# A transformer-block kernel: the identity made on GpSimd, query weights in finer slices, transposes moved by one matmul, and one queue's order fixed

## The chip, the cores and the metric

The kernel runs on one core of one Trainium2 chip. The metric is device time in microseconds (us) of one execution. Every run was in the fast state, with a mean granted TensorE clock of 0.999 to 1.000; only the start is at half of it. "Engine names" below are those of the profile: PE is TensorE's matmul, PEld its weight load, DVE is VectorE, ACT is ScalarE, POOL is GpSimd and SP is SyncE, whose queue issues most loads. Times inside an execution count from the start of the profiled span; one execution takes about 1.8 us longer than its span.

## The reference, cut to what matters

A block in bf16 over 2048 tokens of width 1024: a layer norm, attention over 8 keys at a stride of 2 with 32 heads, a residual, then a second layer norm and a gated MLP with a spatial mix.

```python
def _A_ref(x, wqkv, wo):                       # x (1, 2048, 1024), wqkv (1024, 3072)
    qkv = (x @ wqkv) ...                       # queries, keys, values; 32 heads of 32
    ...                                        # 8 keys at distances 0, 2, .., 14; softmax
    return o @ wo
def _B_ref(x, w_in, w_sp, b_sp, w_out): ...    # gelu, layer norm, spatial mix, product
x = A_x
h = x + _A_ref(_layernorm(x, axis=-1), A_wqkv, A_wo)
h2 = h + _B_ref(_layernorm(h, axis=-1), B_w_in, B_w_sp, B_b_sp, B_w_out)
return h2
```

Its first step: normalize x, multiply by the query part of `wqkv`, then by the key part, then by the value part.

## The kernel before

The tokens are cut into 16 tiles of 128 (`x tile 0` to `x tile 15`) and four chunks of four tiles. In the first chunk each tile is loaded, normalized on VectorE, transposed on TensorE (eight 128x128 transposes against an identity matrix), copied from PSUM to SBUF by ScalarE and then multiplied by wq in 16 matmuls of 512 columns. After the queries of the four tiles come the key matmuls and the value matmuls of the chunk. What the change touches:

```python
NWARM = 11
XAT = (12, 13, 10, 0)       # the next tile's transposes go in front of this matmul of tile 0, 1, 2
...
csb = cpool.tile([P, 416], BF16, name="csb")
dma_w(csb[:, 0:128], consts_d.ap()[:, 0:128])          # dma_w: a load issued by GpSimd
ident = csb[:, 0:128]
...
wps = ps_att.tile([P, CH], FP32, name="wps", tag="L")  # 11 matmuls on zeros, to get the clock up
for _ in range(NWARM):
    T.matmul(wps[:], warm[:, 0:P], warm[:], start=True, stop=True)
...
dma(xts[0][:, 0:CH], x2d[0:P, 0:CH])                   # dma: a load issued by SP
A.dma_start(xts[0][:, CH:D], x2d[0:P, CH:D])           # and by ScalarE
A.dma_start(xts[1], x2d[P:2 * P, :])
for k0 in range(0, KT, 2):                             # wq: four loads of two slices, 512 KB each
    dma(wsb[0][:, k0:k0 + 2, :], wq_view[:, k0:k0 + 2, 0:D])
load_x(2)
load_x(3)
dma(csb[:, 128:416], consts_d.ap()[:, 128:416])
dma(wsb[1][:], wq_view[:, :, D:2 * D])                 # wk
for i in range(TPC, 2 * TPC):
    load_x(i)
...
def xpose(i, xn, *parts):                              # cut: tile 0's first part shares ring "L" with wps
    ...
            T.transpose(tps[i][:, a, :], xn[:, a * P:(a + 1) * P], ident)
    for k0, k1 in parts:
        A.copy(xnT[0][:, k0:k1, i * P:(i + 1) * P], tps[i][:, k0:k1, :])
...
ln(0)                                                  # stats, sqrt, reciprocal, normalize of tile 0
for part in ((0, 2), (2, 5), (5, KT)):
    xpose(0, xns[0], part)
ln(1)
for i in range(TPC):
    acc = new_acc()
    for n, (nh, kt) in enumerate([(nh, kt) for kt in range(KT) for nh in range(2)]):
        if n == XAT[i] and i + 1 < TPC:
            xpose(i + 1, xns[i + 1], (0, 4), (4, KT))
        T.matmul(acc[:, nh, :], xnT[0][:, kt, i * P:(i + 1) * P], wsb[0][:, kt, nh * CH:(nh + 1) * CH],
                 start=(kt == 0), stop=(kt == KT - 1))
    if i + 2 < TPC:
        ln(i + 2)
    ...
    qt_ = nc.sync.dma_start_transpose(...)             # the query tile, transposed by a DMA on SP's queue
tc.add_manual_dep(dma(wsb[2][:], ...wv...).ins, qt_.ins.name, ...)   # wv behind the query transposes
```

TensorE, ScalarE and VectorE run this part in the order in which it is written. The order of SP's queue is chosen by the scheduler of the framework when the kernel is built.

## Time and profile before

| | value | read from |
|---|---|---|
| time | 723.02 us, median of 3 (722.82 to 723.10) | timed runs |
| span of the profiled run | 720.9 us | the page |
| PE busy | 716.6 us, 99% | the page, part 1 |
| first transpose of x tiles 0, 1, 2, 3 | 6.19, 9.62, 13.74, 17.19 us | timeline of PE |
| first query, key, value matmul | 7.02, 22.39, 36.20 us | timeline of PE |
| landing of the identity | 6.02 us | semaphore events of the DMA |
| landing of wq's four loads | 5.76, 7.31, 8.65, 10.01 us | the same |
| landing of x tile 2 | 10.69 us | the same |

First, busy times (share of the span, number of instructions) and the chain that ended last, from the page of the kernel before:

```profile
PE 716.6 (99%) x3449; PEld 364.2 (51%) x3449; DVE 412.1 (57%) x442; ACT 236.3 (33%) x301; POOL 64.1 (9%) x78
...
PE 99%; DVE 0%; DMA 0%; ACT 0%; issue 0%
```

TensorE is the limit, and it has almost no idle time after the start. Near 203.5 us TensorE waits for VectorE's `oT`, by 0.09 us in this profile.

The chain of waits of the kernel before (start us, duration us, what):

```profile
0.74 2.68 DMA xp<-in_A_x_dram
...
5.54 0.65 DVE xn L253 x2
6.18 0.00 issue
6.19 0.37 PE tp_152 L265 x2
6.56 0.55 PE tpa L265 x6
7.10 2.68 PE acc L303 x12
...
13.90 0.45 PE tpa L265 x8
14.35 0.66 PE acc L303 x3
15.01 0.02 issue
15.02 2.33 PE acc L303 x10
```

The chain passes x tile 0's load and its normalization and then stays on PE. The normalized part was there at 5.88, the last warm-up matmul had drained (ended) at 6.13, and the identity had landed at 6.02. The identity's own load is this line of GpSimd's timeline (start, duration, engine, line, operation, what it waited for):

```profile
1.22 0.70 POOL L168 DMA_DIRECT2D csb<-qt_consts  x1 [0.77 <-POOLq L938]
```

Issued at 1.22, landed at 6.02: 4.8 us on the way.

The only other loss is behind x tile 2's transposes. PE's weight loads there (start, busy us, operation; in brackets the idle time and what ended it):

```profile
13.52 0.65 PEld L265 LDWEIGHTS <-xn 128*128 128x128 bf16 x8
14.13 0.37 PEld L303 LDWEIGHTS <-xnT 128*128 128x128 bf16 x3
15.02 0.98 PEld L303 LDWEIGHTS <-xnT 128*128 128x128 bf16 x6 [0.52 <-ACT xnT L267]
```

Three matmuls of the tile in hand follow the eight transposes (L265); the next weight load belongs to tile 2 and waits for ScalarE's copy of those transposes. The matmul behind it starts 0.193 us later than its predecessor's columns need (512 columns take 0.216 us in these traces). I call it the copy stall.

And two lines of VectorE, the statistics and the normalization of x tile 2:

```profile
10.71 0.69 DVE L241 BATCH_NORM_STATS2 bnst<-xp 128x6 f32<-128x512 bf16 x1 [1.70 <-DMA xp<-in_A_x_dram]
...
12.87 0.55 DVE L253 TENSOR_SCALAR xn<-xp,mv_72,rstd_73 128x1024 bf16<-128x1024 bf16 x1
```

The normalized tile is ready at 13.41.

### The profile page before, as it was taken

How to read it: one execution, taken by the hardware profiler on the slowest of the kernel's cores; microseconds unless marked ns; L12 is line 12 of the kernel's file. 1: busy time of each engine (PE TensorE's matmuls, PEld its weight loads, DVE VectorE, ACT ScalarE, POOL GpSimd, SP SyncE). 2: the span in 40 equal slices, each digit the busy share in tenths (PEclk: the TensorE clock that was granted, in tenths of full speed). 3: DMA queues.
4: the chain of work that ended last, by engine and by line, in shares of the span. 5: the costliest groups of instructions: out<-in, count | busy, mean ns of one | idle time of the engine just before them, and what ended most of it. 6: DMA issues, size and time to landing. Idle time of an engine off the chain costs nothing.

```text
span 720.9 us, 8469 instructions
## 1 busy us (share of the span) xinstructions
PE 716.6 (99%) x3449; PEld 364.2 (51%) x3449; DVE 412.1 (57%) x442; ACT 236.3 (33%) x301; POOL 64.1 (9%) x78
## 2 busy tenths in 40 slices
PE   9999999999999999999999999999999999999998
PEld 4666665666544454445445444444444444444444
DVE  5898699979999999887961203222222222222222
ACT  4398452532447685766725520000000000000000
POOL 0010400012002302201114000000000000000000
PEclk9999999999999999999999999999999999999999
DMA  9986664567662842642337989363016301120002
GB/s 335 266 284 151 203 160 167 165 194 253 240 228 91 247 160 90 237 114 59 147 115 210 269 225 307 142 158 106 30 44 148 115 30 45 37 86 9 1 15 73
DMA packets 119990, 107.35 MB, mean 149 GB/s; under 512 B 72896, under 2 KB 98272, under 8 KB 119952
## 3 DMA queue, kind: packets, MB, share of 16 engines
q1 hardware_dynamic: 110624, 73.95, 34.8%
q0 software_dynamic: 7888, 31.43, 13.0%
q10 hardware_dynamic: 1440, 1.44, 0.8%
q8 instruction: 27, 0.44, 0.2%
q14 instruction: 11, 0.09, 0.0%
HBM read 55.09 MB, written 30.74 MB: 119 GB/s over the span
## 4 chain that ended last, share of the span: by engine, by line
PE 99%; DVE 0%; DMA 0%; ACT 0%; issue 0%
PE acc L901 27%; PE acc L393 21%; PE acc L741 13%; PE acc L791 13%; PE acc L923 13%; PE acc L669 8%; PE acc L303 2%; PE L L501 1%; DMA xp<-in_A_x_dram 0%; PE tpa L265 0%; DVE bnst L241 0%; DVE xn L253 0%; DVE bnst L242 0%; DVE ot L925 0%; PE tp_152 L265 0%; ACT sd_145 L247 0%
## 5 line engine op out<-in xcount | busy, mean ns | idle before, releaser
L741 PEld LDWEIGHTS <-hnT 128*128 128x128 bf16 x512 | 50.0, 98 | 47.3 <-issue 0.4
L923 PEld LDWEIGHTS <-zg 128*128 128x128 bf16 x462 | 45.2, 98 | 51.7
L449 DVE TENSOR_TENSOR prod<-qT,kT 128x4096 bf16<-128x4096 bf16 (+1 forms) x32 | 68.1, 2149 | 3.0 <-DMA kT<-qkv_d_58 1.5
L607 DVE TENSOR_TENSOR prod<-vT,AB 128x4096 bf16<-128x4096 bf16 (+1 forms) x32 | 64.3, 2022 | 0.8
L609 DVE TENSOR_TENSOR oT<-oT,prod 128x4096 bf16<-128x4096 bf16 (+1 forms) x32 | 64.5, 2017 | 0.1
L925 DVE TENSOR_TENSOR ot<-acc,hr 128x1024 bf16<-128x1024 f32 (+2 forms) x18 | 19.9, 1106 | 73.1 <-PE acc L923 73.1
L923 PE MATMUL acc<-wout_a,zg 128*128 128x512 bf16 (+1 forms) x264 | 58.2, 373 | 0.0
L741 PE MATMUL acc<-win_1453,hnT 128*128 128x512 bf16 x256 | 58.2, 379 | 0.0
L393 PE MATMUL acc<-xnT,wk 128*128 128x512 bf16 x256 | 56.3, 379 | 0.0
L791 PE MATMUL acc<-hnT,win_1657 128*128 128x512 bf16 x256 | 56.2, 379 | 0.0
L669 PE MATMUL acc<-wo_sb,oT 128*128 128x512 bf16 x256 | 56.1, 379 | 0.0
L393 PE MATMUL acc<-xnT,wv 128*128 128x512 bf16 x256 | 55.9, 379 | 0.0
L404 ACT CAST stg<-acc 128x1024 bf16<-128x1024 f32 x36 | 36.4, 1010 | 58.4 <-PE acc L393 54.6
L393 PEld LDWEIGHTS <-wk 128*128 128x128 bf16 x256 | 36.9, 145 | 18.6 <-issue 0.4
L393 PEld LDWEIGHTS <-wv 128*128 128x128 bf16 x256 | 37.0, 145 | 18.2
L923 PE MATMUL acc<-wout_b,zg 128*128 128x512 bf16 (+1 forms) x198 | 44.4, 373 | 0.0
L741 PE MATMUL acc<-win_1550,hnT 128*128 128x512 bf16 (+1 forms) x256 | 44.2, 326 | 0.0
L791 PE MATMUL acc<-hnT,win_1663 128*128 128x512 bf16 x192 | 42.4, 379 | 0.0
L393 PE MATMUL acc<-xnT,wq 128*128 128x512 bf16 x192 | 42.2, 379 | 0.0
L797 ACT ACTIVATE z1s<-acc 128x1024 bf16<-128x1024 f32 x28 | 28.5, 1019 | 37.2 <-PE acc L791 32.5
L669 PEld LDWEIGHTS <-oT 128*128 128x128 bf16 x256 | 25.0, 98 | 30.3 <-DVE oT L609 0.4
L791 PEld LDWEIGHTS <-win_1657 128*128 128x128 bf16 x256 | 24.9, 98 | 30.0 <-issue 0.4
(267 smaller groups left out, 969.0 us busy)
## 6 DMA issues: line engine op xcount, KB each, us to landing
z_d<-z1s SPq DMA_DIRECT2D x28, 256.0 KB, 2.6
z1c<-z_d SPq DMA_DIRECT2D x28, 256.0 KB, 2.7
z_d<-u SPq DMA_DIRECT2D x12, 448.0 KB, 2.5
xr<-in_A_x_dram SPq DMA_DIRECT2D x16, 256.0 KB, 2.6
h_d<-hb SPq DMA_DIRECT2D x16, 256.0 KB, 2.0
hr<-h_d SPq DMA_DIRECT2D x16, 256.0 KB, 2.8
out_dram<-ot SPq DMA_DIRECT2D x15, 256.0 KB, 2.0
kT<-qkv_d_58 POOLq DMA_DIRECT2D x3, 1056.0 KB, 8.7
```

The lines of the kernel that those rows point to most:

```text
L393: G["mmins", c, xi, dp] = T.matmul(G[key][:, j, :], wv[:, kt, dl, :], xnT[c][:, kt, :], start=(kt == 0), stop=(kt == KT - 1))
L404: A.copy(stg[:], G[key][:])
L449: V.tensor_tensor(qs[w]["prod"][:, d0:d1], qT[:, d0:d1], kT[:, d0:d1, o:o + CH], op=ALU.mult)
L607: V.tensor_tensor(dst[:, :, sq].rearrange("p d (q s) -> p d q s", q=nq), vv, abb, op=ALU.mult)
L609: V.tensor_tensor(oTs[c][:, :, sq], oTs[c][:, :, sq], pvs[w, q0][:, :, sq], op=ALU.add)
L669: T.matmul(st["acc", il][:, nh, :], oTs[c][:, dl, il * P:(il + 1) * P], wo_sb[:, dl, nh * CH:(nh + 1) * CH], start=(dl == 0), stop=(dl == ...
L741: T.matmul(accf[:, n0:n1], hnTs[c][:, il, kt, :], wins[hf][:, kt, n0:n1], start=(kt == 0), stop=(kt == KT - 1))
L791: T.matmul(G["accy", c, fp][:, j, :].rearrange("p (a b) -> p a b", a=TPC), wt[:, kt, f0 * P:(f0 + 1) * P], hnTs[c][:, :, kt, :], start=(kt ...
L797: A.activation(z1s[:], G["accy", c, fp][:], ACTF.Gelu_apprx_tanh)
L901: m_ = T.matmul(acc[:, j, :], z2sb[a][:, f * P:(f + 1) * P], wspT[:, a, :], start=(a == 0), stop=(a == NT - 1))
L923: T.matmul(acc[:, m0 - n0:m1 - n0], zg[:, f, il * P:(il + 1) * P], wt[:, f0, m0:m1], start=(f == 0), stop=(f == NF - 1))
L925: V.tensor_tensor(ot[:, n0:n1], acc[:, 0:n1 - n0], hr[:, n0:n1], op=ALU.add)
```

## The change

Its intent: make the identity on the chip, so that the first transposes need not wait for a load; have wq's later slices land one by one, so that an earlier start finds its weights; move tile 2's transposes one matmul forward, so that four matmuls cover the copy instead of three; and fix the order of SP's queue by explicit dependences.

```diff
-XAT = (12, 13, 10, 0)
+XAT = (12, 12, 10, 0)
...
-    dma_w(csb[:, 0:128], consts_d.ap()[:, 0:128])
     ident = csb[:, 0:128]
+    nc.gpsimd.memset(ident, 1.0)
+    nc.gpsimd.affine_select(ident, ident, [[-1, P]], ALU.is_equal, 0.0, base=0, channel_multiplier=1)
...
+    def turn(i_, j_):      # i_ comes behind j_ in its queue; no semaphore
+        tc.add_manual_dep(i_.ins, j_.ins.name, ...)
+        return i_
...
-    for k0 in range(0, KT, 2):
-        dma(wsb[0][:, k0:k0 + 2, :], wq_view[:, k0:k0 + 2, 0:D])
+    for k0, k1 in ((0, 2), (2, 4), (4, 5), (5, 6), (6, 7), (7, 8)):
+        dma(wsb[0][:, k0:k1, :], wq_view[:, k0:k1, 0:D])
...
+    wv_load = turn(dma(wsb[2][:], wq_view[:, :, 2 * D:3 * D]), qts[3])      # qts: the four query transposes
...
+                if c == 1:
+                    turn(G["xntr", c], wv_load)      # chunk 1's x transposes behind wv's load
...
+                if c == 0:
+                    turn(i_, G["kvhalo"])
...
-        for i in range(2 * TPC, NT - 2):
-            load_x(i)
-        x_slot(NT - 2)
-        x_slot(NT - 1)
-        dma(pairs[NT // 2 - 1][:], ...)              # only x tiles 14 and 15 in one load
+        for i in range(2 * TPC, 2 * TPC + 2):
+            turn(load_x(i), qts[2])                  # x tiles 8 and 9 behind the third query transpose
+        for i in range(2 * TPC + 2, NT, 2):          # x tiles 10 to 15: two to a load
+            ...
+            turn(dma(pairs[i // 2][:], ...), G["xntr", 1])
```

More of the change, by code (lines that the diff above doesn't have):

```diff
@@ L212, in load_x @@
         x_slot(i)
-        dma(xts[i], x2d[i * P:(i + 1) * P, :])
+        return dma(xts[i], x2d[i * P:(i + 1) * P, :])
+    def turn(i_, j_):
+        tc.add_manual_dep(i_.ins, j_.ins.name, mybir.DependencyInfo(mybir.DependencyClass.NoSync, mybir.DependencyReason.DATA),
+                          reason="order of one queue")
+        return i_
+    qts = []
     manual = {mybir.EngineType.PE, mybir.EngineType.Activation, mybir.EngineType.DVE}
@@ L309 @@
             A.copy(qs0[:, i], acc[:].rearrange("p a b -> p (a b)").rearrange("p (m dl) -> p dl m", dl=DLO))
-            qt_ = nc.sync.dma_start_transpose(att_in[0][0][:, :, i * P:(i + 1) * P], qs0[:, i])
-    tc.add_manual_dep(dma(wsb[2][:], wq_view[:, :, 2 * D:3 * D]).ins, qt_.ins.name,
-                      mybir.DependencyInfo(mybir.DependencyClass.NoSync, mybir.DependencyReason.DATA), reason="load wv behind the query transposes")
+            qts.append(nc.sync.dma_start_transpose(att_in[0][0][:, :, i * P:(i + 1) * P], qs0[:, i]))
+    wv_load = turn(dma(wsb[2][:], wq_view[:, :, 2 * D:3 * D]), qts[3])
     wo_sb = wtile([P, DLO, D], "wo_sb", "wB")
@@ L371, in tr @@
                     xnT[c] = xtp.tile([P, KT, CH], BF16, name="xnT", tag="xnT")
-                nc.sync.dma_start_transpose(xnT[c][:, :, il * P:(il + 1) * P], G["xn", c, il][:].rearrange("s (a p) -> s a p", p=P))
+                G["xntr", c] = nc.sync.dma_start_transpose(xnT[c][:, :, il * P:(il + 1) * P], G["xn", c, il][:].rearrange("s (a p) -> s a p", p=P))
+                if c == 1:
+                    turn(G["xntr", c], wv_load)
             trs.append(dma_op(4.0, tr, [n_] + ([G["qkvlast", c - 2]] if c >= 2 else []), free="xn"))
@@ L400, in ev @@
                         if dp == 3:
-                            dma(qkv_d[xi][:, :, CH - HALO:CH], att_in[0][xi][:, :, CH:CH + HALO])
+                            i_ = dma(qkv_d[xi][:, :, CH - HALO:CH], att_in[0][xi][:, :, CH:CH + HALO])
+                            G.setdefault("kvhalo", i_)
                     else:
@@ L652, in xr_load @@
                 st["xr", k] = bp.tile([P, D], BF16, name="xr", tag="xr", bufs=XRB)
-                dma(st["xr", k][:], x2d[(c * TPC + k) * P:(c * TPC + k + 1) * P, :])
+                i_ = dma(st["xr", k][:], x2d[(c * TPC + k) * P:(c * TPC + k + 1) * P, :])
+                if c == 0:
+                    turn(i_, G["kvhalo"])
         dma_op(0.0, xr_load, [G["avmid", c]])
@@ L822, in x_loads @@
     def x_loads():
-        for i in range(2 * TPC, NT - 2):
-            load_x(i)
-        x_slot(NT - 2)
-        x_slot(NT - 1)
-        dma(pairs[NT // 2 - 1][:], x2d[(NT - 2) * P:NT * P, :].rearrange("(a p) d -> p a d", p=P))
+        for i in range(2 * TPC, 2 * TPC + 2):
+            turn(load_x(i), qts[2])
+        for i in range(2 * TPC + 2, NT, 2):
+            x_slot(i)
+            x_slot(i + 1)
+            turn(dma(pairs[i // 2][:], x2d[i * P:(i + 2) * P, :].rearrange("(a p) d -> p a d", p=P)), G["xntr", 1])
     for c in range(1, NCH):
```

## The prediction

> **What bounds the kernel now.** TensorE alone. The page has PE busy 716.6 of 720.9 us at full clock; the chain of waits is 99% PE. In the trace, the only matmul after 6 us that starts over 0.1 us later than its columns need is one of 0.19 us (14.62 to 15.02, a weight load waiting for ScalarE's copy of x tile 2's transposes). From 22.4 us on TensorE hardly waits. So only the first 22 us can give anything; DVE, ACT and DMA later only have to keep pace.
>
> **What bounds the start (timeline and landings, 0 to 22 us).** Warm-up matmuls keep PE busy until about 5.93. The first normalized part of x tile 0 is ready at 5.88. But the identity, a GpSimd DMA issued at 1.22, lands 4.8 us later, at 6.02; PE's wait on it ends at 6.10, the first transpose starts at 6.19. So it is the last wait, by about 0.15 us. Behind it everything is tight: wq's four landings are 5.76, 7.31, 8.65 and 10.01; their first matmuls start at 7.02, 7.89, 8.76 and 10.07. The last two have 0.10 and 0.06 us of slack, so without the split an earlier start would be lost again.
>
> **What the change does.**
> - Identity by memset and select on GpSimd: takes 4.8 us off the path if done before about 5.9. GpSimd is free from about 0.7. A 128x4 power took it 1.04 us here; I estimate memset and 128x128 select at under 2 us, done by 3. Gain 0.15 us. It also takes 16 packets of 2 KB (84 ns each) out of a saturated DMA stream: later landings 0.08 us earlier.
> - wq's slices 4 to 7 one by one: 0.675 us of data each, landings near 7.9, 8.6, 9.25 and 9.9 for matmuls wanted near 8.6, 9.0, 9.9 and 10.3. No wait. Two more issues of 0.47 us on SP delay the issue of x tiles 2 and 3, but their data queue behind wq anyway (tile 2 landed 10.69, expected 10.6).
> - Tile 2's transposes one matmul (0.216 us) earlier: a fourth matmul then covers the ScalarE copy, and the 0.19 us stall goes. They want to start near 13.36; tile 2's normalized x is ready near 13.33, so they start near 13.45, against 13.74. First matmul of tile 2 near 14.77 instead of 15.02.
> - Order of the SP queue: the instruction lists show the same order; the only differences are paired loads of x tiles 10 to 13 and shifted semaphores. About 0.
>
> **Sum.** The first k matmul moves from 22.39 to about 22.14; the 0.25 us should survive, since VectorE's chain hangs on PE at 65.9 and 153.3 us (it waited 2.3 us for PE) and moves with it. PE waits for VectorE once, 0.08 us at 203.4: a late attention DMA could take some back. 723.02 - 0.25 = 722.77.
>
> **Would show it right:** first transpose near 6.0 with no wait for an identity; no excess between matmuls at 8.6 to 10.4; no stall after tile 2's transposes; last matmul 0.25 us earlier.
>
> **What would make it wrong.** The select follows a reconfiguration of GpSimd. The Trainium skill (GPSIMD Engine Reference, 2.1 Instruction dispatch) puts the first call of a freshly loaded kernel at about 6 us of invisible load; in this trace 21 us passed between reconfiguration and first call, so it shows neither yes nor no. If paid, the identity is ready near 7.5 and the kernel is 1 to 1.5 us slower (about 724.3); I give that 15%. Otherwise jitter of attention's DMAs, 0.2 us. Nothing reaches 2%.

## The result, and the profile after

The changed kernel took 722.64 us (median of 6 runs, 722.38 to 722.82), the kernel before 722.96 us in the same rounds (6 runs, 722.81 to 723.12). The ratio of the two is 0.9995 with a 95% interval of 0.9982 to 1.0008: "same" at the 2% level, as predicted. A ratio here is the mean time of one kernel's fast runs over the mean of the other's in the same rounds, so it is not quite the ratio of the medians that are quoted. The interval is wide beside what we look for; I use the means of several sets as well. In this set they differ by 0.34 us; in the repeat below, by 0.37 us. The two ranges of the first set do not overlap, so a gain of about a third of a microsecond looks real. 723 us hold 2000 times that, so this study is about where tenths of a microsecond go.

GpSimd's timeline of the changed kernel:

```profile
0.79 0.20 POOL L169 MEMSET csb<- 128x128 bf16 x1 [0.29 <-POOLq L951]
1.07 0.29 POOL L170 TENSOR_SCALAR_AFFINE_SELECT csb<-csb 128x128 bf16<-128x128 bf16 x1
```

The identity is finished at 1.36 instead of 6.02. The load of GpSimd's code that the prediction feared is not there: a reconfiguration instruction stands at 0.95, the select starts 0.12 us after it and takes 0.29 us. The Trainium skill (GPSIMD Engine Reference, 2.1 Instruction dispatch) says that the first call of a freshly loaded kernel pays about 6 us with no visible instruction; this trace shows no such time for this instruction. Why, no run here tells.

And yet the first transpose did not come sooner. The chain of the changed kernel:

```profile
5.62 0.65 DVE xn L261 x2
6.26 0.07 issue
6.33 0.39 PE tp_155 L273 x2
...
7.17 2.76 PE acc L311 x12
...
13.83 0.04 issue
13.86 0.62 PE tpa L273 x8
14.48 3.02 PE acc L311 x14
```

The first transpose is at 6.33, against 6.19. The trace names the reason: the first transposes share the PSUM buffer "L" with the warm-up matmuls, the warm-up drained at 6.18, and PE's wait on its own semaphore is recorded at 6.22 to 6.27. Tile 2's transposes start at 13.86, against 13.74 before. PE's weight loads and VectorE at the same place as shown of before:

```profile
13.86 0.45 PEld L273 LDWEIGHTS <-xn 128*128 128x128 bf16 x8 [0.53 <-DVE xn L261]
14.27 0.59 PEld L311 LDWEIGHTS <-xnT 128*128 128x128 bf16 x4
15.16 0.77 PEld L311 LDWEIGHTS <-xnT 128*128 128x128 bf16 x5 [0.30 <-ACT xnT L275]
```

```profile
11.10 0.69 DVE L249 BATCH_NORM_STATS2 bnst<-xp 128x6 f32<-128x512 bf16 x1 [2.01 <-DMA xp<-in_A_x_dram]
...
13.26 0.55 DVE L261 TENSOR_SCALAR xn<-xp,mv_73,rstd_74 128x1024 bf16<-128x1024 bf16 x1
```

The copy stall is gone: four weight loads follow the transposes, and the matmul at 15.16 starts when its predecessor allows (the 0.30 us of idle weight load are hidden behind a running matmul). But there is a new wait in front of the transposes: 0.53 us on the weight-load side, 0.198 us of it not hidden, for the normalized tile 2. That tile was loaded at 11.08. So the first profile says that the changed kernel is *later* at 22 us (first key matmul 22.54, before 22.39), while the times say that it is faster. The profiled executions themselves took 722.67 us (kernel before, under the lowest of its timed runs) and 722.79 us (changed kernel, above its median), so the two profiles show a quick execution of the one beside a slow one of the other. One profile of each kernel cannot settle tenths of a microsecond; repeats had to show what varies.

### The profile page after: what moved, and what is told of

It is laid out like the page before. It is cut to its first block, busy times and chain, and to the rows that moved or that the text cites. A ratio compares the mean times of both kernels' runs of the same rounds, so it can differ in the third digit from the quotient of the medians.

```text
span 721.1 us, 8406 instructions
## 1 busy us (share of the span) xinstructions
PE 713.3 (99%) x3388; PEld 364.0 (50%) x3449; DVE 412.1 (57%) x442; ACT 236.3 (33%) x301; POOL 62.3 (9%) x79
## 4 chain that ended last, share of the span: by engine, by line
PE 98%; issue 0%; DVE 0%; DMA 0%; ACT 0%
PE acc L914 27%; PE acc L402 21%; PE acc L803 13%; PE acc L753 13%; PE acc L936 13%; PE acc L681 8%; PE acc L311 2%; PE L L511 1%; DMA xp<-in_A_x_dram 0%; PE tpa L273 0%; DVE bnst L249 0%; DVE xn L261 0%; DVE bnst L250 0%; DVE ot L938 0%; PE tp_155 L273 0%
```

## The experiments

Eleven runs were made (nine variants, and both kernels again), in three sets on three chips, each in five rounds beside the kernel before. All were correct. Where I give a mean below, it is that of the five runs; their scatter is mostly about 0.2 us (standard deviation), so a mean is good to about 0.1 us, which is an estimate from that scatter. Apart from the first result, the changed kernel was in the first of the three sets alone, so most comparisons with it go across sets. Each variant has one profile, which is of one of its five runs, often the quickest or the slowest.

| kernel | median us | mean us | the kernel before, mean of the same set | ratio, 95% interval |
|---|---|---|---|---|
| before, repeated | 723.13 | 723.12 | 722.96 | 1.0002, 0.9990 to 1.0015 |
| changed, repeated | 722.55 | 722.59 | 722.96 | 0.9995, 0.9983 to 1.0008 |
| changed, identity loaded again | 722.69 | 722.82 | 722.96 | 0.9999, 0.9985 to 1.0012 |
| changed, without the fixed order | 723.96 | 724.12 | 722.96 | 1.0016, 1.0004 to 1.0029 |
| changed, tile 2's transposes at 13 again | 722.55 | 722.65 | 722.97 | 0.9997, 0.9984 to 1.0011 |
| changed, wq in four loads again | 722.88 | 722.86 | 722.97 | 0.9999, 0.9987 to 1.0012 |
| changed, warm-up in another buffer | 722.69 | 722.64 | 722.97 | 0.9996, 0.9984 to 1.0009 |
| changed, x tile 2 loaded in halves | 722.90 | 722.86 | 722.97 | 0.9999, 0.9987 to 1.0012 |
| changed, 13 warm-up matmuls | 722.57 | 722.58 | 723.05 | 0.9994, 0.9980 to 1.0008 |
| before, tile 2's transposes at 12 | 722.76 | 723.09 | 723.05 | 1.0001, 0.9988 to 1.0013 |
| changed, three steps more (below) | 722.22 | 722.24 | 723.05 | 0.9989, 0.9976 to 1.0001 |

### 1. Both kernels again

No edit. The labels are `before_again` and `after_again`.

> The kernel before, unchanged, as a control. Every theory: the same as the kernel before within 0.1 us. Its profile is a second sample of the start: how far the landings of x tile 0 (3.42 us in the first profile), the first two wq slices (5.76) and x tile 2 (10.69), and the start of the first k matmul (22.39), move from one execution to the next. If they move by 0.2 us or more, one profile can't settle differences of that size in the start.

> The changed kernel, unchanged. Its first profile showed the first transpose 0.15 us after the last warm-up matmul had drained (6.18 to 6.33), where the kernel before had 0.06 us (6.13 to 6.19), and x tile 2 landing at 11.08 instead of 10.69. Theory 1 (the prediction: the identity's landing was the last wait): the first transpose comes near 6.0 in this second profile. Theory 2 (rival: the last warm-up matmul is the last wait, because the transposes write the PSUM tile that the warm-up wrote): again about 0.15 us after the warm-up has drained, near 6.3. Time: 0.2 to 0.4 us below the kernel before.

Measured: 723.13 and 722.55 us (medians). The control missed its expectation of 0.1 us: its mean, 723.12, is 0.16 us above that of the same kernel in the same set (722.96), so a difference of that size between two means says little. The repeat of the kernel before found the identity landing at 6.64 instead of 6.02, the first transpose at 6.78 instead of 6.19 and the first key matmul at 22.94 instead of 22.39. So in this execution the identity really was the last wait, by half a microsecond (the warm-up had drained at 6.13); in the first profile the warm-up was at least as late. Landings of loads move by 0.6 us between executions of one kernel: wq's first load came at 5.76 in one and 6.42 in the other, x tile 2 at 10.69 and 11.26. The clock varies too: in the first profile of the kernel before the full clock is granted from 6.87 on, behind tile 0's transposes, which are slow there (0.83 us from the first of them to the first query matmul, 0.74 us in the repeat).

The repeat of the changed kernel had its warm-up done at 5.41, because the clock rose earlier, and its first transpose at 6.09, right behind the normalized part (6.04). But tile 2's transposes began at 13.96, and the chain of waits now names their cause itself:

```profile
4.42 6.75 DMA xp<-in_A_x_dram
11.18 0.02 issue
11.20 0.69 DVE bnst L249
...
13.36 0.56 DVE xn L261
13.92 0.05 issue
13.96 0.62 PE tpa L273 x8
```

This chain no longer passes PE's start at all. It comes from x tile 2's load (issued at 4.42, landed at 11.18) through the normalization to the transposes. That gave the theory that the next experiments test. I call it **the gate**: tile 2's transposes start at the later of two times.

- The gate: x tile 2's landing plus 2.79 us. The 2.79 us are the path on VectorE and ScalarE in the changed kernel: 13.86 minus 11.08.
- TensorE's own pace: the first query matmul plus 6.49 us of work (6.71 us where the transposes go in front of matmul 13, one matmul of 0.216 us more), plus TensorE's waits on the way.

The rival: the start passes to the end one to one, and the differences are what each part of the change saves on TensorE.

### 2. The identity loaded again

```diff
-    nc.gpsimd.memset(ident, 1.0)
-    nc.gpsimd.affine_select(ident, ident, [[-1, P]], ALU.is_equal, 0.0, base=0, channel_multiplier=1)
+    dma_w(csb[:, 0:128], consts_d.ap()[:, 0:128])
```

> The changed kernel with the identity loaded by GpSimd's DMA again; its queue order stays fixed. Theory 1: the first transpose waits for the landing near 6.0 to 6.1, and the kernel is 0.15 us slower than the changed one. Theory 2: the identity lands before the warm-up has drained and is not waited for; the first transpose comes near 6.2, no later than in the changed kernel, and the time is the same as the changed kernel's within 0.1 us, if anything lower.

Measured: 722.69 us median, 722.82 mean; 0.21 us above the changed kernel's mean (722.61, over its 11 runs). In the profile the identity landed at 6.46, behind the end of the warm-up at 5.92, and the first transpose waited for it and started at 6.60: theory 2 fails here. That is half a microsecond behind that of the changed kernel's repeat (6.09). The first key matmul, however, is at 22.50, no later than the changed kernel's 22.54 and 22.64: TensorE's pace gives 7.33 + 6.49 = 13.82 and the gate 10.97 + 2.79 = 13.76. The two meet, so half a microsecond at the start was worth next to nothing in that execution. What the identity is worth on average is about 0.2 us by the means, hardly more than the 0.16 us that separate two means of one kernel.

### 3. The fixed order taken away

The kernel before with the on-chip identity, the finer slices and matmul 12, but with none of the `turn` calls and without the paired loads of x tiles 10 to 13.

> The changed kernel without the fixed order of the SP queue and without the paired loads of x tiles 10 to 13. The built program then puts x tiles 8 and 9 before the third query transpose and one transpose of chunk 1 before the fourth query transpose and before the load of wv. The prediction (order worth about 0, as it compared only the two whole kernels' orders): same as the changed kernel within 0.1 us. Rival: the order is what the on-chip identity costs if nothing holds it; wv is issued 1 to 3 us later than 25 us, TensorE (which wants wv near 36.3) waits for it, or VectorE's attention starts later than 27.3; slower than the changed kernel by 0.5 to 3 us.

Measured: 723.96 us median, 724.12 mean: 1.51 us above the changed kernel's mean, the largest effect, and slower than the kernel before. Its start is like the changed kernel's (first transpose 6.12, first key matmul 22.59). Its profile is of the slowest of its five runs (724.95 us; the others took 723.68 to 724.16), so the sizes below are those of the worst case: 1.9 us in front of the value matmuls, and 0.35 us more at the very end, as in experiment 7. The loss comes later. SP's queue in this kernel, then in the changed kernel (start, busy us, operation):

```profile
24.06 1.01 SPq L214 DMA_DIRECT2D xp<-in_A_x_dram  x2
26.38 1.24 SPq L373 DMA_TRANSPOSE xnT<-xn  x1
27.72 1.28 SPq L311 DMA_TRANSPOSE qT<-qs  x1
29.05 0.58 SPq L312 DMA_DIRECT2D wv<-in_A_wqkv_dram  x1
```

```profile
24.03 1.24 SPq L318 DMA_TRANSPOSE qT<-qs_215  x1
25.32 0.57 SPq L319 DMA_DIRECT2D wv<-in_A_wqkv_dram  x1
26.36 10.58 SPq L379 DMA_TRANSPOSE xnT<-xn  x4
```

Without the dependences, two loads of later x tiles and one transpose of chunk 1 stand in front of the fourth query transpose, and wv's load, which follows that one, is issued at 29.05 instead of 25.32. It takes 9.1 us to land in both. PE then has to wait; its first value matmul of this kernel:

```profile
38.23 1.95 PE L394 MATMUL acc<-xnT,wv 128*128 128x512 bf16 x8 [1.67 <-DMA wv<-in_A_wqkv_dram]
```

The same place in the changed kernel:

```profile
36.35 3.83 PE L402 MATMUL acc<-xnT,wv 128*128 128x512 bf16 x17
```

What moved the queue is the identity: in the kernel before, the built order is that of the changed kernel, but building (not running) the kernel before with nothing changed except the on-chip identity gives the bad order of this experiment. The scheduler takes another decision when one load is replaced by two GpSimd instructions. (The paired loads were taken away in this run together with the dependences; the two were not run apart.) So the fixed order is not a gain of its own; it is what the other parts need in order to keep theirs.

### 4. Tile 2's transposes at matmul 13 again, and at 12 in the kernel before

```diff
-XAT = (12, 12, 10, 0)
+XAT = (12, 13, 10, 0)
```

> The changed kernel with tile 2's transposes after 13 matmuls again. Prediction: the stall of about 0.19 us behind ScalarE's copy comes back and the kernel is 0.19 us slower than the changed one. Theory 3 (new: in the changed kernel tile 2's transposes wait for VectorE's normalized tile, that is for x tile 2's landing plus 2.75 us, and this gate sets everything after it): the thirteenth matmul fills a wait that is there anyway; the stall shows in the trace, but the first k matmul stays within 0.1 us of 22.6 and the time within 0.1 us of the changed kernel's.

Measured: 722.65 us mean, 722.55 median: no different from the changed kernel. The weight loads show why:

```profile
13.61 0.45 PEld L273 LDWEIGHTS <-xn 128*128 128x128 bf16 x8 [0.46 <-DVE xn L261]
14.02 0.37 PEld L311 LDWEIGHTS <-xnT 128*128 128x128 bf16 x3
14.91 0.98 PEld L311 LDWEIGHTS <-xnT 128*128 128x128 bf16 x6 [0.52 <-ACT xnT L275]
```

The copy stall is back (0.193 us), but the wait in front of the transposes is shorter, 0.128 us, since one more matmul fills it. Together that is 0.32 us. At matmul 12 it would have been 0.128 + 0.216 = 0.34 us in front and nothing behind. The same time is lost in another place. The first key matmul was at 22.28, and not within 0.1 us of 22.6 as expected: this profile is of the quickest of the five runs (722.40 us), in which x tile 2 landed early, at 10.83.

The opposite experiment puts this one part alone into the kernel before:

```diff
-XAT = (12, 13, 10, 0)
+XAT = (12, 12, 10, 0)
```

> The kernel before with x tile 2's transposes moved by one matmul (12 instead of 13) and nothing else. Theory: in the kernel before TensorE's own pace reaches tile 2 (the stall of 0.19 us behind the copy of its transposes is in series), so the stall goes and the move is worth 0.1 to 0.2 us there: tile 2's first transpose 6.5 us after the first query matmul, no excess at the matmul behind the transposes, 722.8 to 722.9. Rival (the gate of x tile 2's landing plus 2.8 us is already nearly closed in the kernel before): a new wait in front of tile 2's transposes takes what the stall gives back, and the time is the same as before, 722.95 to 723.05.

Measured: 722.76 us median; one of its five runs took 724.47 us, for which no profile tells the cause, and which spoils the mean (723.09 beside 723.05 for the kernel before; the other four average 722.74). The times alone do not show a gain; the profile does. In the profile the stall is gone and no wait came in its place: tile 2's transposes start 6.50 us behind the first query matmul, and the first key matmul 15.17 us behind it, against 15.37 and 15.43 in the two profiles of the kernel before. So in the kernel before, in this profile, the step is worth about what its 0.19 us stall says, because the gate had opened (14.07) just before TensorE came (14.11); in the changed kernel no gain is seen.

### 5. wq in four loads again

```diff
-    for k0, k1 in ((0, 2), (2, 4), (4, 5), (5, 6), (6, 7), (7, 8)):
-        dma(wsb[0][:, k0:k1, :], wq_view[:, k0:k1, 0:D])
+    for k0 in range(0, KT, 2):
+        dma(wsb[0][:, k0:k0 + 2, :], wq_view[:, k0:k0 + 2, 0:D])
```

> The changed kernel with wq in four loads of two slices. Prediction: the matmuls of slices 4 and 6 wait for landings near 9.15 and 10.5, and the whole gain of the start is lost: slower than the changed kernel by 0.15 us. Theory 3: the same waits, but up to 0.4 us of them is hidden before the gate of tile 2; TensorE reaches tile 2's transposes near 14.15 where the gate opens near 13.9, so 0.2 to 0.3 us slower. If the split were worth nothing: same within 0.05 us and no wait at slices 4 and 6.

Measured: 722.86 us mean, 0.25 us above the changed kernel, in the range that theory 3 had given. PE's timeline shows the wait that the prediction expected without the split, at the first matmul of slice 4:

```profile
9.04 1.02 PE L311 MATMUL acc<-wq,xnT 128*128 128x512 bf16 x4 [0.33 <-DMA wq<-in_A_wqkv_dram]
```

By the starts of the matmuls it cost 0.50 us, and with two smaller waits at slices 2 and 6 it is 0.62 us. Up to tile 2 nearly all of that is hidden: without the waits TensorE would have been there at 6.74 + 6.49 = 13.23, the gate opened at 11.02 + 2.79 = 13.81, and the transposes started at 13.84, not near 14.15 as theory 3 had it. The first key matmul is at 22.50, no later than in the two profiles of the changed kernel (22.54 and 22.64). This execution was slow (723.04 us) for other reasons: 0.31 us of it were lost far behind the start, where TensorE's weight loads waited for VectorE, and 0.10 us at the end.

```profile
203.79 2.27 PEld L681 LDWEIGHTS <-oT 128*128 128x128 bf16 x12 [0.62 <-DVE oT L619]
```

So the wait for wq is shown, but not that it is what costs the 0.25 us of the means; that stays open.

### 6. The warm-up in another PSUM buffer

```diff
-    wps = ps_att.tile([P, CH], FP32, name="wps", tag="L")
+    wps = ps_acc.tile([P, CH], FP32, name="wps", tag="acc")
```

> The changed kernel with the warm-up matmuls in a PSUM tile of the accumulators' ring, so that the first transposes no longer wait for the last warm-up matmul to drain. All theories: the first transpose comes within 0.1 us of the first normalized part of tile 0 (near 6.0 to 6.1), never at 6.3. If the start sets the time (prediction): up to 0.2 us faster than the changed kernel. Theory 3: the first k matmul stays near 22.6, the time the same within 0.1 us.

Measured: 722.64 us mean, no different from the changed kernel. The profile is of the quickest run (722.30 us). The wait on PE's own semaphore is gone, and the first transpose starts at 6.07, 0.06 us behind the normalized part, though the warm-up drained at 6.05, nearly as late as in the first profile of the changed kernel. That is an earlier start, and in this execution the gate was the later limit: x tile 2 landed at 10.70, and its transposes started at 13.49 = 10.70 + 2.79, 0.17 us behind TensorE's pace. The first key matmul was at 22.16, not near 22.6 as theory 3 had said, because the tile landed early here. The times do not decide against the rival: in an execution like the changed kernel's repeat, where the warm-up ends before the normalized part is there, this edit has nothing to take away.

### 7. x tile 2 loaded in halves

```diff
-    load_x(2)
+    x_slot(2)
+    for n0 in (0, CH):
+        dma(xts[2][:, n0:n0 + CH], x2d[2 * P:3 * P, n0:n0 + CH])
```

The first statistics instruction needs only the first half, so the gate should open earlier.

> The changed kernel with x tile 2 loaded as two halves of 512 columns, so that VectorE's statistics can begin on the first half about 0.34 us before the second has landed (half of the 0.68 us that 256 KB take). Theory 3: tile 2's normalized x is ready 0.3 us earlier (near 13.55), its transposes start then or when TensorE gets there, the first k matmul moves to 22.3 to 22.4 and the kernel is 0.2 to 0.35 us faster than the changed one. If the start sets the time: tile 2's transposes come no earlier, same time.

Measured: 722.86 us mean, no gain; this expectation of the theory was missed. The halves landed at 10.95 and 11.31, so the chain behind the tile was shortened by those 0.36 us, and tile 2's transposes started at 13.73, the first half plus 2.78. But the whole stream of loads was late in this execution: TensorE waited 0.49 us for wq's third slice, which landed at 7.85, and 0.13 us more for later ones, so the pace alone would have brought it to 6.54 + 6.49 + 0.62 = 13.65. What the theory lacked is that the tile's load is the last of one stream, and that the loads in front of it can be late as well. The first key matmul, at 22.41, was nevertheless earlier than in both profiles of the changed kernel, and the last store landed earlier too (719.90, against 720.17 and 720.13); what made this execution slow (722.98 us) is that its span ended 1.33 us behind that landing instead of 0.91. Why the other four runs were slow stays open, as they have no profile.

### 8. Two more warm-up matmuls: a late start on purpose

```diff
-NWARM = 11
+NWARM = 13
```

> The changed kernel with 13 warm-up matmuls instead of 11: the start is delayed on purpose. Theory (the gate): two more matmuls at the slow clock are 0.43 us each, so the first transpose starts up to 0.85 us later, at about 7.0 us, or less if the clock rises during the warm-up; of that the wait in front of tile 2's transposes absorbs up to 0.4 us, so the first key matmul is at 22.5 to 22.9 and the time 0.1 to 0.5 us over the changed kernel, 722.7 to 723.1. Rival (the start passes to the end one to one): 0.6 to 0.85 us over, 723.2 to 723.5.

Measured: 722.58 us mean, not slower than the changed kernel. Neither the rival's 723.2 to 723.5 nor the theory's 722.7 to 723.1 came about. In the profile, again of the quickest run (722.46 us), the experiment did not do what it was meant to do: the clock rose early (the warm-up's seventh matmul, at 3.83, was the first shorter one), the 13 warm-up matmuls were done at 5.59 and the first transpose started at 5.94. The start was not late, so this run does not test the rival. The gate is seen again: x tile 2 landed at 10.82, the transposes started at 13.61 = 10.82 + 2.79, 0.39 us behind TensorE's pace. How late the start was in the other four runs is not known, so of the timed runs I claim only that nothing was lost. The first key matmul was at 22.28, earlier than the 22.5 to 22.9 expected.

### 9. Three steps more

If the gate binds, x tile 2 has to land earlier, and what TensorE needs in between has to be needed later. This version loads tile 2 ahead of wq's last slice, interleaves the query matmuls of tiles 0 and 1 so that wq's last slices are used later, and has the warm-up in the other buffer.

```diff
-    wps = ps_att.tile([P, CH], FP32, name="wps", tag="L")
+    wps = ps_acc.tile([P, CH], FP32, name="wps", tag="acc")
...
-    for k0, k1 in ((0, 2), (2, 4), (4, 5), (5, 6), (6, 7), (7, 8)):
+    for k0, k1 in ((0, 2), (2, 4), (4, 5), (5, 6), (6, 7)):
         dma(wsb[0][:, k0:k1, :], wq_view[:, k0:k1, 0:D])
     load_x(2)
+    dma(wsb[0][:, 7:8, :], wq_view[:, 7:8, 0:D])
...
+        # mms(i, *kts): tile i's query matmuls with wq's slices kts; put(i): what followed them
+        mms(0, 0, 1, 2, 3, 4)
+        xpose(1, xns[1], (0, 4), (4, KT))
+        mms(0, 5, 6)
+        ln(2)
+        mms(1, 0, 1)
+        mms(0, 7)
+        put(0)
+        mms(1, 2, 3, 4, 5)
+        xpose(2, xns[2], (0, 4), (4, KT))
+        mms(1, 6, 7)
+        ...                                  # ln(3), put(1); tiles 2 and 3 as before
```

> The changed kernel with three things more: the warm-up matmuls write a buffer of the accumulation ring instead of the one that the transposes share; x tile 2's load is issued before wq's last slice instead of after it; the query matmuls of x tiles 0 and 1 are interleaved so that wq's slices 5, 6 and 7 are needed later. Theory (the gate: x tile 2's landing plus about 2.8 us opens its transposes, at 13.8 to 14.0 us in the changed kernel): x tile 2 lands about 0.7 us earlier, at about 10.3 to 10.5, the gate opens at about 13.2, TensorE's own pace of 6.49 us from its first query matmul then decides, tile 2's first transpose starts at 13.2 to 13.4, the first key matmul at 22.0 to 22.2, and the time is 722.2 to 722.4, 0.2 to 0.45 us under the changed kernel. Rival (the whole stream of DMA transfers up to x tile 2 binds, not its last transfer): TensorE waits at the first wq slices by what was saved, the key matmuls start at 22.4 or later, and the time is 722.5 to 722.7.

Measured: 722.22 us median, 722.24 mean (722.15 to 722.35), 0.36 us below the changed kernel's mean and 0.81 us below the kernel before in the same set. x tile 2 landed at 10.33, as expected. VectorE, then PE, in this version:

```profile
10.35 0.69 DVE L250 BATCH_NORM_STATS2 bnst<-xp 128x6 f32<-128x512 bf16 x1 [1.19 <-DMA xp<-in_A_x_dram]
...
12.51 0.55 DVE L262 TENSOR_SCALAR xn<-xp,mv,rstd 128x1024 bf16<-128x1024 bf16 x1
```

```profile
7.69 1.46 PE L314 MATMUL acc<-wq,xnT 128*128 128x512 bf16 x6 [0.20 <-DMA wq<-in_A_wqkv_dram]
9.23 0.62 PE L274 MATMUL tpa<-csb,xn 128*128 128x128 bf16 x8
9.68 4.05 PE L314 MATMUL acc<-wq,xnT 128*128 128x512 bf16 x17
13.57 0.61 PE L274 MATMUL tpa<-csb,xn 128*128 128x128 bf16 x8
```

The gate opened at 10.33 + 2.79 = 13.12 and is no longer what binds. TensorE's pace is: it waited 0.36 us for wq's third slice (landed at 7.65) and 0.25 us in front of tile 1's transposes, whose tile landed at 6.51, so that tile 2 began at 6.46 + 6.49 + 0.61 = 13.56, and not at the 13.2 to 13.4 of the expectation; the first key matmul was at 22.23, just outside the 22.0 to 22.2 expected. So the rival named there is half right: the next limit is the stream of loads itself, x tiles 0 and 1 and the first half of wq. The gain was in the range expected, but it came from taking the gate away, with TensorE still 0.6 us short of the pace that it could have. Every timed run of this version was faster than every run of the kernel before in its set (722.35 at most, 722.74 at least); of the changed kernel's eleven runs the quickest (722.32) is just below the slowest of this one, the one profiled. Of the three steps, only the warm-up's buffer was also run alone. The changed kernel was not in the same set; I compare through the kernel before, whose means in the sets are 722.96, 722.97 and 723.05 us.

### The two limits, over all profiles

The later of the two computed times should be the start of tile 2's transposes. Times in us; "waits" are TensorE's waits between the first query matmul and tile 2's transposes, for wq or for tile 1, read from the same profile.

| kernel | first query matmul | + work + waits = pace | tile 2 landed | + 2.79 = gate | transposes start |
|---|---|---|---|---|---|
| before | 7.02 | + 6.71 = 13.73 | 10.69 | 13.48 | 13.74 |
| before, repeated | 7.51 | + 6.71 = 14.22 | 11.26 | 14.05 | 14.29 |
| before, matmul 12 | 7.61 | + 6.49 = 14.10 | 11.28 | 14.07 | 14.11 |
| identity loaded again | 7.33 | + 6.49 = 13.82 | 10.97 | 13.76 | 13.83 |
| wq in four loads | 6.74 | + 6.49 + 0.62 = 13.85 | 11.02 | 13.81 | 13.84 |
| changed | 7.17 | + 6.49 = 13.66 | 11.08 | 13.87 | 13.86 |
| changed, repeated | 6.85 | + 6.49 + 0.22 = 13.56 | 11.18 | 13.97 | 13.96 |
| without the fixed order | 6.88 | + 6.49 + 0.14 = 13.51 | 11.13 | 13.92 | 13.91 |
| x tile 2 in halves | 6.54 | + 6.49 + 0.62 = 13.65 | 10.95 (first half) | 13.74 | 13.73 |
| matmul 13 again | 6.78 | + 6.71 = 13.49 | 10.83 | 13.62 | 13.61 |
| warm-up elsewhere | 6.83 | + 6.49 = 13.32 | 10.70 | 13.49 | 13.49 |
| 13 warm-up matmuls | 6.69 | + 6.49 = 13.18 | 10.82 | 13.61 | 13.61 |
| three steps more | 6.46 | + 6.49 + 0.61 = 13.56 | 10.33 | 13.12 | 13.57 |

Two constants give thirteen starts within 0.07 us (the 2.79 was taken from the changed kernel, the 6.49 from the kernel before with matmul 12). The kernels that load the identity sit on the side of the pace; those that make it on the chip, and have finer slices, sit on the side of the gate, until the last row takes the gate away. The rival, a start that passes to the end one to one, fails in the traces: from the first query matmul to the first key matmul the two profiles of the changed kernel take 15.37 and 15.79 us, and the kernel with the identity loaded again starts its first transpose half a microsecond behind the changed kernel's repeat and yet reaches the first key matmul 0.14 us earlier.

## Why the prediction was right or wrong

The time was right. Predicted were 722.77 us; measured were 722.64. The predicted gain was 0.25 us, measured were 0.34 and 0.37 (differences of means). The way there was right in parts.

- **"TensorE alone" bounds, and only the first 22 us can give anything: right in the main.** The span minus the first key matmul stayed at 698.4 to 698.5 us in ten of the thirteen profiles. The kernel without the fixed order lost its time mostly at 36 us, and single executions lost 0.3 to 0.4 us near 203.8 us or at the very end (experiments 5 and 7). The wait for VectorE near 203 us, which the prediction named with 0.08 us, was 0.13 us in the first profile of the changed kernel.
- **"So it is the last wait, by about 0.15 us": half right.** In the profile that I read, the warm-up's drain (6.13, with the first transpose at 6.19 in the same PSUM buffer) was at least as binding; I had given the warm-up an end of 5.93. In the repeat the identity was the last wait by half a microsecond. The size of the term varies between executions from about nothing to 0.5 us, and one profile could not show it.
- **Identity in under 2 us, done by 3: right**, with room: done at 1.36. The risk of 6 us of hidden load, given 15%, did not come about.
- **"Later landings 0.08 us earlier": not shown.** Landings move by 0.6 us from one execution to the next, which hides it.
- **Finer slices, no wait: right in the first profile; in the repeat, with an earlier start, three small waits of 0.22 us together were left.** Without them the waits are there, 0.62 us in the profile, but the gate hid them; that the 0.25 us of the times come from them is not shown.
- **Tile 2's transposes "start near 13.45", and the 0.19 us stall goes: the step that failed.** The stall went, but the transposes started at 13.86 and 13.96. The prediction had seen how near the normalized tile was ("ready near 13.33"), and took tile 2's landing (10.6) as if it were fixed. It came at 11.08 and 11.18. With the start moved forward, that landing plus 2.79 us is the limit, and no gain of the moved transposes is seen in the changed kernel (722.65 with them undone, 722.61 with them), though in a profile of the kernel before they are worth their stall. Where the tile did land early, at 10.70 with the warm-up in another buffer, the transposes started at 13.49, close to the prediction: the term that was mis-sized is the landing.
- **Order of the queue, "about 0": right as the comparison of the two whole kernels, wrong as a reading of what it is for.** The prediction compared the lists of the two kernels and saw the same order. It did not build the kernel without this part. The on-chip identity alone changes the order, and without the fix (and the paired loads) the kernel is 1.2 us slower than the kernel before instead of 0.35 us faster.
- **First key matmul "near 22.14": not shown.** It was at 22.54 and 22.64 in the two profiles of the changed kernel, and at 22.39 and 22.94 before. By the profiles' means that is 22.59 against 22.67. The scatter of the kernel before, 0.55 us, is larger than the gain; only the timed runs show the gain.

So that the sum was near the truth is in part luck. The likely account, which is argued and not shown for the timed runs, is that its missteps partly cancelled: the start gives more than 0.15 us in the executions in which the identity is late, and the gate then takes back what the moved transposes were to give. Undone one at a time, identity, slices and transposes cost 0.21, 0.25 and 0.04 us (each to about 0.1, and across sets). Their sum of 0.5 cannot be told from the whole gain of 0.35 at that precision. That these terms need not add follows from the two limits of the table, of which the later decides; how the 0.35 us are shared among them in the timed runs is not shown.

## What to carry to other kernels

When a start-up path is shortened, ask at once which load lands next behind it, and compute its own path to TensorE: the later of two nearly equal limits decides, and steps that pass by on the earlier one are worth nothing. Replacing one load can make the scheduler reorder a queue a long way off, so build each part of a change alone and compare the orders, also where the whole change shows the same order. Where landings vary by half a microsecond between executions, read two profiles before a difference of tenths is explained, and look up where the profiled execution's own time lies among the timed runs.

## What the Trainium skill lacked or had wrong

- GPSIMD Engine Reference, 2.1 Instruction dispatch, tells of about 6 us for the first call of a freshly loaded kernel. The affine select, the first of its kind in the program, started 0.12 us behind the reconfiguration instruction and took 0.29 us. The page does not say which instructions are exempt.
- TensorE: Matmul & The Clock Gate, Part 1, What's actually happening, gives a free-running window of 3.4 us, a transition that varies by 500 ns either way, and a note that the number of slow matmuls varies from run to run. The spread here was larger: with the first warm-up matmul at 1.25 to 1.31, the trace grants the full clock from 3.99 us on in the earliest profile (13 warm-up matmuls) and from 7.07 us on in the latest (kernel before, matmul 12). Of the warm-up matmuls, between 6 and all 11 were slow (0.427 us apart, against 0.216 us fast), which fits the note and not the 500 ns.
- DMA: Bandwidth & Descriptors: I found nothing on how far the start of a stream of loads moves from one execution to the next. Here wq's first load landed at 5.76 and at 6.42 in two profiles of the kernel before; the rate moved little: in the changed kernel's two profiles the slices of 256 KB landed 0.66 to 0.69 us apart, about 390 GB/s.
- I found no page on a wait for TensorE's own earlier matmuls when a PSUM buffer is used again: in the changed kernel's first profile TensorE's wait on its own semaphore stands at 6.22 to 6.27, 0.04 us behind the warm-up's drain, and the first transpose started at 6.33; with the warm-up in another buffer it started 0.02 us behind that drain.
